# Cutting the last transform of a GFNet mixer at 94-token units instead of 512-token blocks, with a ring in front of the MLP

## The chip, the cores and the metric

One core of one Trainium2 chip runs the whole program. The metric is the device time of one execution in microseconds (us); lower is better. All numbers come from runs and their traces; where a page of the Trainium skill is drawn on, it is named.

## The reference, cut to what matters

```python
x: (8, 3008, 256)                 # 8 sequences, 3008 tokens, 256 channels
X = rfft(x, axis=1)
y = irfft(X * (filt_r + 1j * filt_i), n=3008, axis=1)      # GFNet mixing
t = y.reshape(24064, 256)
h = t @ w_in                                               # 256 -> 2048
g = h * clip(h + 3, 0, 6) / 6                              # hardswish
out = g @ w_out                                            # 2048 -> 256
```

The kernel computes the transforms as matrix products: 3008 = 47 x 64. The last product of the inverse transform takes one *unit* of 96 coefficients (in the partitions) x 256 channels and gives 94 tokens x 256 channels; a sequence has 32 such units. In the kernel's own token order the 24,064 tokens are 47 blocks of 512 for the MLP, which does its two products by a Strassen-like scheme of seven products. Everything is fp32; one product is two passes on TensorE, so two weight-load records (LDWEIGHTS) and two MATMUL records.

## The kernel before

A step is one of eight slices of the hidden width for one block: 376 steps. In two steps of a block the last transform of the *next* block is done (`n_unit`, one call for each half of the channels). It computes just the 512 tokens of that block, so the units at its edges are cut in two pieces:

```python
TOK = 94; BLK = 512
def pieces(k):                       # unit (b, j), first token r in it, n tokens, place in the block
    t = k * BLK
    while t < (k + 1) * BLK:
        u, r = divmod(t, TOK)
        n = min(TOK - r, (k + 1) * BLK - t)
        yield u // HC, u % HC, r, n, t - k * BLK
        t += n

def n_unit(k, dh):
    if dh == 0:
        st["xn", k] = xnp.tile([P, 2, 512], FP32, name="xn")
    ps = psF.tile([P, 512], FP32, name="psn", tag="f")
    for i, (_, _, r, n, o) in enumerate(pieces(k)):
        nc.tensor.matmul(ps[:, ds(o, n)], t4[k % 2][:, i, ts(dh, P)], wai[:, ds(r, n)], start=True, stop=True)
    x = st["xn", k]
    nc.scalar.activation(out=x[:, dh, :], in_=ps, func=AXT.Copy)
    if dh == 0:
        return
    ...                              # four GpSimd subtractions into xt, for the Strassen-like products

# in a step:                         (... cut)
up_1(k, p)                           # 3 products of 256 columns
do(True)                             # n_unit, or units of the other transforms
down(kd, pd, 1); up_2(k, p)          # 128-column and 256-column products by turns, and so on
```

`t4` is the stationary operand (its 128 columns are loaded for each piece) and `wai`, at most 94 columns, is what streams. `t4_load` brings the units of a block from a scratch tensor in HBM.

## Time and profile before

| what | value |
|---|---|
| median time | 2876.54 us at first, 2875.4 to 2877.6 in later rounds; single runs 2872.7 to 2880.2 |
| span of the profiled run | 2872.3 us |
| TensorE passes, those of the changed stage | 18,280, 1208 |
| bytes moved by DMA | 216.47 MB |
| first pass of the changed stage | at 135.7 us |

The prediction shows and reads the main lines. Names for the rest: a *pass* is one LDWEIGHTS with its MATMUL; of the tiles that TensorE writes, `psn` is that of the changed stage, `psf` those of the other transforms, `al` and `be` those of the MLP's first product and `po` that of its second.

### The profile page before, as it was taken

The page shows a single profiled execution, that of the slowest core. Times are in us where ns is not written, and L with a number is a line of the kernel's source. Part 1 is how long each engine was busy: PE and PEld are TensorE (multiplying, and loading weights), DVE is VectorE, ACT ScalarE, POOL GpSimd, SP SyncE. Part 2 cuts the span into 40 slices and gives each one's busy share as a digit, 9 for nine tenths or more (in the row PEclk, how much of TensorE's full clock was granted, in tenths as well). Part 3 has the DMA queues.
Part 4 walks back from the last instruction along what each step waited for, and adds up shares of the span by engine and source line. Part 5 has one row for each costly group of instructions (what it writes and reads, how often), then busy time and mean ns, then how long its engine had stood idle before and what let it go on. Part 6 is the DMA issues. An engine that isn't in the chain of part 4 may idle for free.

```text
span 2872.3 us, 47938 instructions
## 1 busy us (share of the span) xinstructions
PE 2745.6 (96%) x18280; PEld 2487.8 (87%) x18280; DVE 1991.8 (69%) x3492; ACT 1326.2 (46%) x2622; POOL 508.7 (18%) x836
## 2 busy tenths in 40 slices
PE   4569999999999999999999999999999999999997
PEld 1358988999989998899988999899998999999996
DVE  3697876677757776577766777667775677766665
ACT  1124445444454445544445444554445444444443
POOL 3274013200131001310023000321013100000000
PEclk9689999999999999999999999999999999999998
DMA  6543312421133222331223221242213421110100
GB/s 204 158 121 104 95 49 79 114 75 53 54 88 104 65 59 71 85 104 58 65 73 95 79 85 39 83 110 74 61 42 88 121 64 55 30 34 19 31 8 15
DMA packets 129036, 216.47 MB, mean 75 GB/s; under 512 B 26088, under 2 KB 87336, under 8 KB 128808
## 3 DMA queue, kind: packets, MB, share of 16 engines
q1 hardware_dynamic: 99784, 151.50, 18.6%
q0 software_dynamic: 23552, 55.62, 6.6%
q10 hardware_dynamic: 5472, 6.29, 0.6%
q8 instruction: 145, 2.38, 0.3%
q14 instruction: 83, 0.68, 0.1%
HBM read 138.33 MB, written 74.97 MB: 74 GB/s over the span
## 4 chain that ended last, share of the span: by engine, by line
PE 90%; DVE 4%; DMA 3%; POOL 1%; issue 1%; SPq 1%; ACT 1%; ACTq 0%; POOLq 0%; DVEq 0%
PE po L417 40%; PE al L341 22%; PE be L341 16%; PE psn L326 4%; PE psf L257 3%; PE psf L285 3%; PE psf L231 2%; DMA z_tmp<-t 1%; SPq L453 0%; DVE g L391 0%; DVE s L271 0%; DMA out_dram<-o 0%; DVE s L270 0%; POOL z_tmp L245 0%; DMA bits<-in_moe_w_out_dram 0%
## 5 line engine op out<-in xcount | busy, mean ns | idle before, releaser
L417 PEld LDWEIGHTS po<-w_out,g 128*128 128x128 f32 x10528 | 1408.8, 192 | 145.8 <-DVE g L399 31.3
L417 PE MATMUL po<-w_out,g 128*128 128x128 f32 x10528 | 1434.5, 277 | 25.8 <-DVE g L391 25.2
L386 ACT ACTIVATE r<-h,half_c 128x512 f32<-128x512 f32 x752 | 542.6, 722 | 341.8 <-DVE h L367 329.5
L391 DVE SCALAR_TENSOR_TENSOR g<-r,h 128x512 f32<-128x512 f32 x752 | 517.6, 688 | 257.0 <-ACT r L386 243.9
L341 PE MATMUL al<-xt,w_in 128*128 128x256 f32 x2256 | 677.4, 382 | 3.7 <-DVE h L372 2.1
L367 DVE TENSOR_TENSOR h<-be,s 128x512 f32<-128x512 f32 x376 | 259.8, 691 | 309.0 <-PE be L341 279.6
L341 PE MATMUL be<-xn,w_in 128*128 128x256 f32 x1504 | 447.8, 379 | 0.0
L341 PEld LDWEIGHTS al<-xt,w_in 128*128 128x128 f32 x2256 | 343.9, 193 | 6.8 <-issue 3.1
L341 PEld LDWEIGHTS be<-xn,w_in 128*128 128x128 f32 x1504 | 286.1, 190 | 38.9
L381 ACT ACTIVATE h<-al 128x256 f32<-128x256 f32 x376 | 144.4, 384 | 376.9 <-PE al L341 376.9
L372 DVE TENSOR_TENSOR h<-al,s 128x256 f32<-128x256 f32 x376 | 159.6, 425 | 193.1 <-PE al L341 192.8
L245 POOL DMA_DIRECT2D z_tmp<-t x448 | 226.2, 513 | 375.5 <-ACT t L234 366.9
L399 DVE TENSOR_TENSOR g<-g 128x512 f32<-128x512 f32 x376 | 262.6, 699 | 12.9
L362 ACT ACTIVATE s<-al 128x256 f32<-128x256 f32 x376 | 144.5, 384 | 201.9 <-PE al L341 201.9
L353 ACT ACTIVATE s<-be 128x256 f32<-128x256 f32 x376 | 144.4, 384 | 181.0 <-PE be L341 181.0
L341 PE MATMUL al<-xn,w_in 128*128 128x256 f32 x752 | 225.3, 381 | 0.5 <-ACT h L381 0.5
L341 PE MATMUL be<-xt,w_in 128*128 128x256 f32 x752 | 224.1, 380 | 0.0
L352 ACT ACTIVATE s<-al 128x256 f32<-128x256 f32 x376 | 144.4, 384 | 70.5 <-PE al L341 70.5
L398 DVE TENSOR_TENSOR g<-g 128x256 f32<-128x256 f32 x376 | 164.0, 436 | 12.8
L401 DVE TENSOR_TENSOR g<-g 128x256 f32<-128x256 f32 x376 | 161.0, 428 | 12.8
L326 PEld LDWEIGHTS psn<-wai,t 128*128 128x128 f32 x1208 | 152.0, 194 | 15.3 <-issue 10.6
L341 PEld LDWEIGHTS be<-xt,w_in 128*128 128x128 f32 x752 | 143.2, 190 | 19.4
(50 smaller groups left out, 1760.6 us busy)
## 6 DMA issues: line engine op xcount, KB each, us to landing
z_tmp<-t POOLq DMA_DIRECT2D x448, 48.0 KB, 2.1
t<-z_tmp SPq DMA_DIRECT2D x42, 512.0 KB
g_tmp<-t POOLq DMA_DIRECT2D x42, 512.0 KB, 3.4
xs<-in_x_dram SPq DMA_DIRECT2D x128, 128.0 KB
out_dram<-o SPq DMA_DIRECT2D x328, 47.0 KB
t<-g_tmp SPq DMA_DIRECT2D x96, 144.0 KB
ft<-in_filt_r_dram SPq DMA_DIRECT2D x96, 128.0 KB
ft<-in_filt_i_dram SPq DMA_DIRECT2D x96, 128.0 KB
```

Source lines behind the costliest of these rows:

```text
L245: q.dma_start(z[:, h, ds(c * XC + 2 * g, 2), :], t[p0:p0 + KH, h, :, :])
L326: nc.tensor.matmul(ps[:, ds(o, n)], t4[k % 2][:, i, ts(dh, P)], wai[:, ds(r, n)], start=True, stop=True)
L341: nc.tensor.matmul(ps, w_in[p][:, w, :], x, start=start, stop=stop, skip_group_check=True)
L362: nc.scalar.activation(out=s[:, 1, :], in_=al, func=AXT.Copy)
L367: nc.vector.tensor_tensor(out=st["h"][0].rearrange("p (a n) -> p a n", a=2), in0=be, in1=s, op=ALU.add)
L372: nc.vector.tensor_tensor(out=st["h"][1][:, 256:512], in0=al, in1=s5, op=ALU.add)
L386: nc.scalar.activation(out=r, in_=st["h"][i], func=AXT.Relu, bias=half_c, scale=1.0 / 6.0)
L391: nc.vector.scalar_tensor_tensor(out=st["g", k, p][:, o:o + 2, :].rearrange("p a n -> p (a n)"), in0=st["r", i], scalar=1.0, in1=st["h"][i ...
L398: v.tensor_tensor(out=g[:, G1, :], in0=g[:, G3, :], in1=g[:, G22, :], op=ALU.add)
L399: v.tensor_tensor(out=g[:, G3:G2 + 1:2, :], in0=g[:, G3:G1 + 1, :], in1=g[:, G11:G11 + 1, :].broadcast_to([P, 2, 256]), op=ALU.subtract)
L401: v.tensor_tensor(out=g[:, G4, :], in0=g[:, G12, :], in1=g[:, G2, :], op=ALU.subtract)
L417: nc.tensor.matmul(st["po", k][bank][:, part, u, :], g[:, a, ts(u, P)], w_out[p][:, w, :], start=(p == 0 and n in OPENS and u == 0), stop= ...
```

## The change

Its intent: cut at unit edges, so that no unit is loaded as weights twice, and let the MLP take its blocks of 512 out of a ring of three blocks into which chunks of up to five units (470 columns, within the 512 of a PSUM tile) are copied.

```diff
+NJ = 5
+RING = 3 * BLK
-    t4 = [const.tile([P, 7, D], FP32, name="t4%d" % i) for i in range(2)]
+    t4 = [const.tile([P, NJ, D], FP32, name="t4%d" % i) for i in range(2)]
+    xn = const.tile([P, 2, RING], FP32, name="xn")
 ...
+    chunks = [(b, j, min(NJ, HC - j)) for b in range(B) for j in range(0, HC, NJ)]
+    def n_unit(i, dh):
         ps = psF.tile([P, 512], FP32, name="psn", tag="f")
-        for i, (_, _, r, n, o) in enumerate(pieces(k)):
-            nc.tensor.matmul(ps[:, ds(o, n)], t4[k % 2][:, i, ts(dh, P)], wai[:, ds(r, n)], start=True, stop=True)
-        x = st["xn", k]
-        nc.scalar.activation(out=x[:, dh, :], in_=ps, func=AXT.Copy)
+        for q in range(chunks[i][2]):
+            nc.tensor.matmul(ps[:, ts(q, TOK)], t4[i % 2][:, q, ts(dh, P)], wai, start=True, stop=True)
+        t, n = token(i)
+        done = 0
+        while done < n:
+            o = (t + done) % RING
+            m = min(n - done, RING - o)
+            nc.scalar.activation(out=xn[:, dh, ds(o, m)], in_=ps[:, ds(done, m)], func=AXT.Copy)
+            done += m
+        if dh and (t + n) // BLK > t // BLK:
+            t_sums(t // BLK)                       # the four subtractions, as before
 ...
-        t4_load(0); t4_load(1)                     # (written here in one line)
-        for dh in range(2):
-            n_unit(0, dh)
+        for i in range(2):
+            t4_load(i)
+        for i in range(2):
+            for dh in range(2):
+                n_unit(i, dh)
 ...                                                # and the plan of the later chunks:
+            n_at[i] = s = (k - 1) * NP + (6 if head or k in used else 3)
+            at(max(stored, n_at[i - 2] + 1), t4_load, i)
```

The MLP's products read `xn[:, d, ts(k % 3, BLK)]`; the output stores are cut at the same places as before.

More of the change, by code (lines that the diff above doesn't have):

```diff
@@ L107 @@
     t3p = pool("t3p", 2)
-    xnp = pool("xnp", 2)
+    xtp = pool("xtp", 2)
     rp = pool("rp", 2)
@@ L292, in g_store @@
         q.dma_start(g_d[b, ts(c, TC), :, :].rearrange("k p d -> p k d"), st.pop(("t3", b, c)))
-    def pieces(k):
-        t = k * BLK
-        while t < (k + 1) * BLK:
-            u, r = divmod(t, TOK)
-            n = min(TOK - r, (k + 1) * BLK - t)
-            yield u // HC, u % HC, r, n, t - k * BLK
-            t += n
-    def t4_load(k):
-        slot = 0
-        found = []
-        for b, j, _, _, _ in pieces(k):
-            if found and found[-1][0] == b:
-                found[-1][2] += 1
-            else:
-                found.append([b, j, 1])
-        for b, j, n in found:
-            for h in range(2):
-                for ri in range(2):
-                    p0 = h * 64 + ri * 32
-                    nc.sync.dma_start(t4[k % 2][p0:p0 + KH, slot:slot + n, :],
-                                      g_d[b, :, ds(ri * NC + h * HC + j, n), :])
-            slot += n
@@ L321, in n_unit @@
-    def n_unit(k, dh):
-        if dh == 0:
-            st["xn", k] = xnp.tile([P, 2, 512], FP32, name="xn")
-        ps = psF.tile([P, 512], FP32, name="psn", tag="f")
-        for i, (_, _, r, n, o) in enumerate(pieces(k)):
-            nc.tensor.matmul(ps[:, ds(o, n)], t4[k % 2][:, i, ts(dh, P)], wai[:, ds(r, n)], start=True, stop=True)
-        x = st["xn", k]
-        nc.scalar.activation(out=x[:, dh, :], in_=ps, func=AXT.Copy)
-        if dh == 0:
-            return
-        t = xnp.tile([P, 4, 256], FP32, name="xt")
-        b11, b12, b21, b22 = (x[:, d, ts(h, 256)] for d in range(2) for h in range(2))
+    chunks = [(b, j, min(NJ, HC - j)) for b in range(B) for j in range(0, HC, NJ)]
@@ new lines, in token, with t4_load @@
+    def token(i):
+        b, j, n = chunks[i]
+        return b * N + j * TOK, n * TOK
+    def t4_load(i):
+        b, j, n = chunks[i]
+        for h in range(2):
+            for ri in range(2):
+                p0 = h * 64 + ri * 32
+                nc.sync.dma_start(t4[i % 2][p0:p0 + KH, 0:n, :], g_d[b, :, ds(ri * NC + h * HC + j, n), :])
+    def n_unit(i, dh):
+        ps = psF.tile([P, 512], FP32, name="psn", tag="f")
+        for q in range(chunks[i][2]):
[9 more added lines that the diff above has]
+            t_sums(t // BLK)
@@ L333, in n_unit, with xb, t_sums @@
+    def xb(k, d):
+        return xn[:, d, ts(k % 3, BLK)]
+    def t_sums(k):
+        t = xtp.tile([P, 4, 256], FP32, name="xt")
+        b11, b12, b21, b22 = (xb(k, d)[:, ts(h, 256)] for d in range(2) for h in range(2))
         for o, x0, x1 in ((0, b12, b11), (1, b22, t[:, 0, :]), (2, b22, b12), (3, b21, t[:, 1, :])):
@@ L343, in up_1 @@
     def up_1(k, p):
-        x, t = st["xn", k], st["xt", k]
+        t = st["xt", k]
         al = psU.tile([P, 256], FP32, name="al")
@@ L348, in up_1 @@
         s5 = hp.tile([P, 256], FP32, name="s5")
-        product(al, p, A11, x[:, 0, 0:256], start=True)
+        product(al, p, A11, xb(k, 0)[:, 0:256], start=True)
         product(be[:, 1, :], p, S1, t[:, 0, :], start=True)
-        product(be[:, 0, :], p, A12, x[:, 1, 0:256])
+        product(be[:, 0, :], p, A12, xb(k, 1)[:, 0:256])
         nc.scalar.activation(out=s[:, 0, :], in_=al, func=AXT.Copy)
@@ L356, in up_2 @@
     def up_2(k, p):
-        x, t = st["xn", k], st["xt", k]
+        t = st["xt", k]
         al, be, s, s5 = st["up"]
@@ L360, in up_2 @@
         product(al, p, S2, t[:, 1, :])
-        product(be[:, 1, :], p, S4, x[:, 1, 256:512], stop=True)
+        product(be[:, 1, :], p, S4, xb(k, 1)[:, 256:512], stop=True)
         nc.scalar.activation(out=s[:, 1, :], in_=al, func=AXT.Copy)
@@ L448, in out_5 @@
         o = st.pop(("o", k))[0].rearrange("p t u d -> p (t u) d")
-        for b, j, r, n, t in pieces(k):
-            while n:
-                h, a = divmod(r, NA)
-                m = min(NA - a, n, P - t % P)
-                nc.sync.dma_start(raw(out, b * N + a * NC + h * HC + j, [[NC * D, m], [1, D]]),
-                                  o[t % P:t % P + m, t // P, :])
-                r, t, n = r + m, t + m, n - m
+        t, end = k * BLK, (k + 1) * BLK
+        while t < end:
+            b, r = divmod(t, N)
+            j, r = divmod(r, TOK)
+            h, a = divmod(r, NA)
+            p = t % P
+            m = min(NA - a, P - p)
+            nc.sync.dma_start(raw(out, b * N + a * NC + h * HC + j, [[NC * D, m], [1, D]]),
+                              o[p:p + m, t % BLK // P, :])
+            t += m
     first = [b * N // BLK for b in range(B)]
@@ L514 @@
                         t2_load(0, c + TB, nc.gpsimd)
-        t4_load(0)
-        t4_load(1)
-        for dh in range(2):
-            n_unit(0, dh)
+        for i in range(2):
[3 more added lines that the diff above has]
+                n_unit(i, dh)
         for c in range(3):
@@ L523 @@
             at(i // 2, convert, 1)
-        for k in range(1, NBLK):
-            s = (k - 1) * NP
-            if k not in first:
-                if k > 1:
-                    at(s - 4, t4_load, k)
-                for dh in range(2):
-                    at(s + 3 + dh, n_unit, k, dh)
-            else:
-                at(s + (3 if k > first[1] else 4), t4_load, k)
-                for dh in range(2):
-                    at(s + 6 + dh, n_unit, k, dh)
+        n_at = {0: -2, 1: -2}
+        used = {}
+        stored = 0
+        for i in range(2, len(chunks)):
+            k = token(i)[0] // BLK
+            head = chunks[i][1] == 0
+            n_at[i] = s = (k - 1) * NP + (6 if head or k in used else 3)
+            used[k] = 1
+            if head:
+                stored = s - 3 + (k == first[1])
+            at(max(stored, n_at[i - 2] + 1), t4_load, i)
+            for dh in range(2):
+                at(s + dh, n_unit, i, dh)
         def places(n):
```

## The prediction

> **What bounds the kernel now.** I read the page's busy shares and slices first, then the windows of busy time by stage, then the waits of TensorE, then the groups with different shapes kept apart, and last the timeline and the chain around one run of the stage that is changed.
>
> ```profile
> PE 2745.6 (96%) x18280; PEld 2487.8 (87%) x18280; DVE 1991.8 (69%) x3492; ACT 1326.2 (46%) x2622; POOL 508.7 (18%) x836
> ...
> PE   4569999999999999999999999999999999999997
> ```
>
> TensorE is busy almost everywhere; the other engines have slack on average. The windows say where "almost" ends (columns: length, then busy us and instructions of each engine, granted clock, DMA share, GB/s).
>
> ```profile
> 0.00:142.00 142.00, 66.72 (x187) 33.89 (x188) 75.68 (x124) 18.33 (x31) 43.16 (x61) 0.85 0.61 182
> 142.00:217.00 75.00, 51.92 (x260) 38.69 (x258) 66.19 (x110) 21.95 (x44) 56.26 (x82) 0.82 0.42 121
> 217.00:1000.00 783.00, 776.35 (x5235) 707.68 (x5232) 558.41 (x973) 379.01 (x750) 145.20 (x249) 1.00 0.28 81
> 1000.00:2000.00 1000.00, 999.64 (x6789) 915.00 (x6787) 702.12 (x1239) 491.87 (x974) 170.52 (x296) 1.00 0.27 77
> 2000.00:2765.00 765.00, 765.00 (x5224) 711.60 (x5223) 531.47 (x944) 373.74 (x742) 89.25 (x144) 1.00 0.19 53
> ```
>
> Three stages: a prologue up to 142 us (the first sequence's transform) with TensorE half idle; 142 to 217 us, where VectorE is busy 66 of 75 us (it still converts the weights) and TensorE waits; and everything after, where TensorE has no idle time worth the name (7 us before 1000, 0.4 us from 1000 to 2765). From 217 us on a TensorE pass removed is time removed, and a wait appears only if something is made later by more than its slack. That DVE L391 is what TensorE waits for in the middle stage is shown by the waits of TensorE: 21.5 us there, 3.7 us after.
>
> The changed stage is the last inverse transform (`n_unit`), whose output `psn` feeds the MLP:
>
> ```profile
> L326 PE MATMUL psn<-wai,t 128*128 128x94 f32 x840 | 115.0, 283 | 9.7 <-DMA t<-g_tmp 9.7
> ...
> L326 PE MATMUL psn<-wai,t 128*128 128x10 f32 x8 | 1.2, 224 | 0.0
> ```
>
> (The last line is not needed for a sum; it shows what the change removes: 10-column products.) 1208 records are 604 products of two passes each. 840 passes have the full 94 columns, 368 are pieces cut by the 512-token block edge. What a pass costs is not its own duration (283 ns, pipelined) but the distance to the next start. The chain of waits, in time order, shows whole groups:
>
> ```profile
> 135.71 5.32 PE psn L326 x24
> ...
> 504.03 1.46 PE psn L326 x14
> ...
> 674.18 1.27 PE psn L326 x12
> ```
>
> Reading single starts inside them: full 94-column passes start every 111 to 112 ns, exactly as the 128-column passes of `po` do (mean 113); the distances of a group with pieces 92, 94, 94, 94, 94, 44 are 79, 112, 113, then 112 eight times apart from one 59 ahead of the last. So two narrow passes come some 30 to 80 ns cheaper per group, the others cost a weight load each, whatever their width.
>
> **What the Trainium skill says.** "TensorE: Matmul & The Clock Gate", section "LDWEIGHTS (loading the stationary operand)": a load takes about its column count over 1.2 GHz, and that is 107 ns for 128 columns; the trace's 111.5 ns agrees within 5 ns and explains why the width hardly matters. The same page's "Back-to-back issue gap" gives some 81 ns for a load and matmul pair at 128 columns; for these fp32 passes the trace has 112 to 113, and I use the trace. Its Part 1 on the clock gate says that a cold TensorE runs at half rate until about one window (3.4 us) of sustained work: the trace has a granted clock of 0.5 from 120.9 to 144.8 us, and the 24 passes at 135.7 us at 213 ns each; here the release came only 9 us after TensorE had begun. "Perfetto Trace Analysis", "Identifying the Most-Contended Engine", warns that matmul occupancy isn't closeness to the limit; that is why the 96% is not used as a measure and starts are.
>
> **The change part by part.**
>
> 1. *Cuts at units in place of blocks.* Each sequence's 32 units of 94 tokens go in chunks of 5, 5, 5, 5, 5, 5, 2: 56 chunks, 512 products, 1024 passes, all 94 wide. That is 184 passes fewer. The passes of blocks 1 to 46 took, start of group to start of what follows, 52 groups of 12 at 1.29 us and 40 of 14 at 1.49 us, 127.5 us in sum. Of this 0.6 us is one wait for a load and 0.75 us (8 times 0.09) belongs to the 64-row products that follow some groups: they cost the same extra after an MLP product. Left: 126.2 us. A new group of 10 passes should take 81 (its first, from the 79 of a 92-wide one) plus 9 x 112 = 1.09 us; a group of 4 passes 81 + 3 x 112 = 0.42 us. After the prologue there are 46 five-unit chunks and 8 two-unit ones, two groups (halves of D) each: 92 x 1.09 + 16 x 0.42 = 106.8 us. **Gain 19.4 us**, of which the two groups near 184 and 199 us (0.6 us) lie where VectorE is the bound and are worth nothing.
>
> 2. *Prologue.* Two chunks instead of one block must be done before the first MLP product: 40 passes in place of 24, at the cold 213 ns. **Loss 16 x 0.213 = 3.4 us.** It doesn't come back when block 1 needs less, because the next 70 us hang on VectorE, whose conversions begin behind the first MLP step and move with it. The second chunk's load is issued right behind the first (0.4 us per issue, four issues), so it should land during the first 4.3 us of passes.
>
> 3. *Evictions.* 94 ScalarE copies of 512 columns become 142: 112 chunk halves, 30 of them cut in two where the ring wraps (15 of 56 chunks). 512 columns take 597 ns and 256 take 384, so 171 ns are fixed; columns in sum are the same; 48 x 0.171 = 8.2 us more ScalarE work. ScalarE is 46% busy, a wrap delays one copy by 0.17 us, and the next copy that TensorE needs (`s`, L362) comes over a microsecond later. **0 us.**
>
> 4. *Loads.* 302 unit slots become 256, each 96 rows of 1 KB: 4.5 MB less of 216, in 224 issues instead of 216. DMA share is 0.2 to 0.3. The load of a chunk is issued as soon as its buffer is free (up to 15 steps ahead, formerly 7); a sequence's first chunk still comes 3 steps ahead. **0 us**, perhaps the 0.6 us of the one late load.
>
> 5. *GpSimd sums.* Still 188 subtractions. In ten blocks rather than seven they follow one step, about 7 us, ahead of use; they need a copy (0.6 us) and four times 0.73 us, 3.5 us. **0 us.**
>
> Sum: -19.4 + 0.6 + 3.4 = -15.4 us. 2876.5 - 15.4 = **2861 us**, 0.5% less.
>
> **Rivals.** (a) *A new wait in the ring.* Products of a block read what was written by up to two chunks, and a chunk overwrites the block two behind. If the dependencies were kept for the ring as a whole and not by region, each of 54 chunks could stall TensorE for a copy plus sums, some 3 to 5 us: +150 us or more, slower. Against it: the instruction order of the changed kernel shows the MLP's products waiting for no more semaphores than before, and the overwritten block was last read a step or more before the write. (b) *The late sums or the early loads stop an in-order queue.* SyncE now waits in its queue for the passes that free a buffer, and output stores and loads stand behind it; GpSimd issues `z_tmp` stores, eight in 4 us, beside the sums. If each of the 3 extra late blocks lost 2 us and a dozen loads 1 us, the gain would be nearly eaten: about 2872 to 2876. Against it: the old kernel has seven such blocks and no TensorE wait on GpSimd after 217 us, and the waiting loads stand in the queue less than a step. (c) *Fewer passes, same time*, if another engine were the true bound in the steps with `n_unit`. Steps without it run through with no TensorE gap, so the shorter step isn't caught by VectorE; I give this little. (d) *A prologue that hides its extra passes*: if the clock is released earlier, the loss is 1.8 us rather than 3.4 and the time 2859.
>
> **Range and chances.** The mechanism is counted, not guessed; what is unsure is the prologue (2 us each way), waits of a few us under (b), and the scatter of runs (2876.2 to 2879.9 before). I take 2855 to 2868. Faster by over 2% would need 58 us, three times all that can be removed; slower by over 2% needs (a).
>
> **What would show it.** TensorE records 18,096 in place of 18,280, all `psn` passes 94 wide and 1024 of them. `psn` groups of 10 in the chain with about 1.07 to 1.09 us, and none of 12 or 14. The prologue's passes as 40 in about 8.5 us, and the first MLP product near 144 rather than 141 us. ScalarE busy near 1334 us, GpSimd's count unchanged. TensorE idle after 217 us still under 10 us, with no GpSimd releaser. A larger idle sum naming `xn` copies or `xt` sums would make (a) or (b) right and the prediction wrong; groups of ten that take under 1.0 us or over 1.2 would break step 1.

## The result, and the profile after

Median 2857.90 us (2856.28 to 2859.84, 4 runs) against 2877.61 us (2876.24 to 2879.91, 4 runs): 19.7 us less. The ratio is 0.9931 (95% interval 0.9914 to 0.9948). The time lies in the predicted range, 3 us below the 2861 us foretold.

The page of the changed kernel, first its span and then its busy times:

```profile
span 2854.4 us, 47635 instructions
...
PE 2726.7 (96%) x18096; PEld 2469.4 (87%) x18096; DVE 1995.0 (70%) x3492; ACT 1331.6 (47%) x2670; POOL 511.7 (18%) x836
...
DMA packets 129323, 211.92 MB, mean 74 GB/s; under 512 B 26184, under 2 KB 87240, under 8 KB 129096
```

184 passes fewer, 48 ScalarE instructions more, GpSimd with the same count, 4.55 MB less moved: the counts that were foretold. (ScalarE is 5.4 us busier.) The groups of the last transform, shapes kept apart, and the waits of TensorE from 217 us on (columns: us in total, times, longest):

```profile
L316 PE MATMUL psn<-wai,t 128*128 128x94 f32 x1024 | 133.0, 278 | 9.2 <-DMA t<-g_tmp 9.2
```

```profile
PE po L417 <- DVE g L391: 4.1, 3, 2.5
PE al L341 <- DVE h L372: 2.1, 4, 1.2
PE psf L260 <- DVE s L274: 0.4, 1, 0.4
PE po L417 <- DVE o L443: 0.3, 1, 0.3
```

One shape is left where there were 47, and no wait on the ring's copies, on GpSimd or on a load appeared. The same list of the kernel before has 7.5 us in these stretches, this one 6.9; a wait of 0.4 us for a late `t4` load is gone. Its longest lines:

```profile
PE po L417 <- DVE g L391: 3.7, 3, 2.1
PE al L341 <- DVE h L372: 1.4, 3, 0.8
PE al L341 <- ACT s L362: 1.0, 1, 1.0
PE psf L257 <- DVE s L271: 0.4, 1, 0.4
PE psn L326 <- DMA t<-g_tmp: 0.4, 1, 0.4
```

The chain of waits, in time order, around one group after the change (start, length, what):

```profile
673.55 0.86 PE be L341 x4
674.41 1.09 PE psn L316 x10
675.50 0.47 PE po L417 x4
675.97 0.43 PE al L341 x2
```

A group of ten passes takes 1.09 us, as the prediction had it. The prologue, by windows of the trace (columns as in the prediction's windows), first before, then after:

```profile
135.70:140.80 5.10, 5.09 (x24) 5.10 (x25) 0.00 (x0) 0.60 (x1) 0.72 (x1) 0.50 0.85 190
140.80:144.80 4.00, 4.00 (x16) 2.15 (x15) 0.00 (x0) 1.36 (x3) 2.09 (x3) 0.50 0.47 111
144.80:149.30 4.50, 2.91 (x13) 1.28 (x9) 2.18 (x5) 2.50 (x6) 0.00 (x0) 1.00 0.29 86
```

```profile
136.70:145.30 8.60, 8.58 (x40) 8.60 (x41) 0.00 (x0) 1.69 (x3) 0.72 (x1) 0.50 0.81 204
145.30:146.10 0.80, 0.80 (x4) 0.71 (x4) 0.00 (x0) 0.52 (x1) 0.00 (x0) 0.53 0.31 65
146.10:152.20 6.10, 4.52 (x22) 2.10 (x21) 2.19 (x5) 3.32 (x9) 2.10 (x3) 1.00 0.52 143
```

The 24 passes became 40 and 5.1 us became 8.6, at the granted clock of 0.50 throughout. But the first MLP step, which ran 4.0 us at half clock before, now does so for 0.7 us only: 8.47 us from its first product to the next step's have become 6.84. (These are two single traces. Others of the same prologue have up to 3.6 us at half clock; see split_copies below.)

**A ruler for the rest.** The profiled runs of all these kernels differ by up to 5 us in when the changed stage begins, which is scatter of the part before it. So the trace is read in two stretches that don't contain it. The *head* goes from the first `psn` pass to the first MLP product of block 2 (step 16); the *body* from there to the start of the last TensorE pass. Both are differences of starts.

| kernel | head us | body us |
|---|---|---|
| before | 164.7 | 2550.9 |
| after | 166.7 | 2530.1 |
| change | +2.0 | -20.9 |

With the stage beginning 1.0 us later in this one run (136.7 against 135.7) that is the whole 17.9 us by which the two spans differ. The body repeated to 0.01 us in another run of the same kernel (2530.07), so tenths of a microsecond can be read from it.

### The profile page after: what moved, and what is told of

Same layout as the page of the kernel before. It is cut to its first block, busy times and chain, and to the rows that moved or that the text cites. A ratio compares the mean times of both kernels' runs of the same rounds, so it can differ in the third digit from the quotient of the medians.

```text
span 2854.4 us, 47635 instructions
## 1 busy us (share of the span) xinstructions
PE 2726.7 (96%) x18096; PEld 2469.4 (87%) x18096; DVE 1995.0 (70%) x3492; ACT 1331.6 (47%) x2670; POOL 511.7 (18%) x836
## 4 chain that ended last, share of the span: by engine, by line
PE 91%; DVE 5%; DMA 2%; issue 1%; ACT 1%; ACTq 0%; SPq 0%; POOL 0%; POOLq 0%; DVEq 0%
PE po L417 41%; PE al L341 22%; PE be L341 17%; PE psn L316 4%; PE psf L260 3%; PE psf L288 3%; PE psf L234 2%; DMA z_tmp<-t 1%; DVE g L391 0%; DVE s L183 0%; DVE s L192 0%; DVE s L194 0%; DVE s L181 0%; DVE g L398 0%; DVE s L274 0%
## 5 line engine op out<-in xcount | busy, mean ns | idle before, releaser
L334 POOL TENSOR_TENSOR xt<-xn 128x256 f32<-128x256 f32 x94 | 72.0, 766 | 508.1 <-ACT xn L322 508.0
```

## The experiments

The theory after the result: the gain is the number of passes, each worth one weight load of about 112 ns whatever its width; the prologue's extra passes cost something that is given back in part; copies, loads and sums cost nothing. All twelve kernels gave right results. The first four of the table, the next four, the next three and the last were each timed together, in five rounds, against nine runs of the kernel before; each of these batches ran on another chip, so medians are best compared within one, ratios across them.

| run | median us | ratio to before (95%) | head us | body us |
|---|---|---|---|---|
| after_again | 2856.61 | 0.9935 (0.9921 to 0.9948) | 166.7 | 2530.1 |
| add_passes | 2877.08 | 1.0007 (0.9995 to 1.0020) | 166.3 | 2549.4 |
| wide | 2853.87 | 0.9926 (0.9913 to 0.9938) | 163.8 | 2530.3 |
| long_head | 2865.76 | 0.9968 (0.9955 to 0.9980) | 176.5 | 2530.1 |
| split_copies | 2860.18 | 0.9936 (0.9924 to 0.9949) | 167.4 | 2530.5 |
| late_load | 2858.16 | 0.9938 (0.9925 to 0.9952) | 167.4 | 2530.1 |
| spread | 2857.72 | 0.9937 (0.9925 to 0.9950) | 167.5 | 2530.0 |
| spread_short | 2856.39 | 0.9926 (0.9914 to 0.9939) | 165.0 | 2529.6 |
| short_head | 2856.55 | 0.9931 (0.9918 to 0.9943) | 165.2 | 2529.6 |
| warm | 2855.63 | 0.9928 (0.9915 to 0.9940) | 161.6 | 2530.1 |
| warm_short | 2854.18 | 0.9923 (0.9910 to 0.9937) | 161.6 | 2529.6 |
| warm6_short | 2855.84 | 0.9924 (0.9910 to 0.9937) | 165.7 | 2529.6 |

**The base, once more.**

> The changed kernel once more, as the base for the runs beside it: 2856 to 2860 us, ratio to the kernel before 0.993.

2856.61 us, as expected.

**Is it the passes?** The number of passes is put back, and nothing else:

```diff
+        if i >= 2 and chunks[i][2] == NJ:
+            nc.tensor.matmul(ps[:, ts(NJ - 1, TOK)], t4[i % 2][:, NJ - 1, ts(dh, P)], wai, start=True, stop=True)
```

> Each five-unit group after the prologue repeats its last product: 92 products, 184 passes, as many as the change removed, all 94 wide, and nothing else. Theory (a pass costs one weight load, 112 ns): +184 x 0.112 = +20.6 us over the changed kernel, about 2878 us, so the whole gain is gone. Rival (the gain comes from better placed loads, evictions or sums, and passes are partly free): under +10 us.

The page of that run:

```profile
PE 2747.9 (96%) x18280; PEld 2490.1 (87%) x18280; DVE 1994.4 (69%) x3492; ACT 1329.8 (46%) x2670; POOL 509.2 (18%) x836
```

The pass count is that of the kernel before, and so is the time: 20.5 us more than after_again against 20.6 expected. In the body 176 of them stand, and it grew by 19.4 us: 110 ns each. The rival, that loads, copies or sums had brought the gain, falls: with all of those as in the changed kernel, the gain is gone.

**Is it the pass or its columns?** `wai` is padded with zeros to 128 columns and the next product overwrites what is too much:

```diff
-            nc.tensor.matmul(ps[:, ts(q, TOK)], t4[i % 2][:, q, ts(dh, P)], wai, start=True, stop=True)
+            nc.tensor.matmul(ps[:, ds(q * TOK, WID)], t4[i % 2][:, q, ts(dh, P)], wai, start=True, stop=True)   # WID = 128
```

> Each product runs over 128 columns in place of 94, 34 of them zeros that the next product overwrites; counts are the same. Theory (a pass costs its weight load, the width only shows in the first pass of a group): 108 groups x 28 ns = +3.0 us over the changed kernel. Rival (a pass costs its columns): 34/94 of some 107 us = +39 us.

Neither came. The rival's 39 us fall at once: 36% more columns cost 0.3 us in the body. But the theory's +3.0 us are a miss too. The groups did become 28 ns longer each, `psn` 2.9 us in the body, and the products *behind* them became shorter by 2.6 us (the `po` 1.9, the `psf` of the forward transform 0.7). And the whole run was 2.7 us faster: the head is 2.9 us shorter. Two things to explain, then; the next experiments do so.

**The 81 ns of a group's first pass.** In a group the first distance is 81 ns and the others 112. If that were a load hidden behind the 256-column pass ahead of it, then putting each product behind such a pass should pay:

```diff
+    def n_parts(i, dh):                      # the products of n_unit, one at a time, then the copy
 ...
         product(al, p, S2, t[:, 1, :])
+        next_part()
         product(be[:, 1, :], p, S4, xb(k, 1)[:, 256:512], stop=True)
+        next_part()
 ...                                          # and behind up_1 or an early unit, behind S3, behind A22
```

> The products of a chunk half stand one by one behind the 256-column MLP products of a step, in place of five in a row (not in the ten blocks whose sums follow one step ahead of use). If a pass behind a 256-column pass costs 81 ns because its load is hidden there, and the others 112, a five-product group of 1.09 us becomes five pieces of 0.19 us: 0.12 us less each, 82 groups, about -10 us against the changed kernel, 2848 us. Rival (the 81 ns is a matter of the record of the first pass alone, the load is not hidden): 0 us.

No gain: 2857.72 us, a body of 2530.0 us. The chain of waits in time order shows both sides of the account; in the first five rows the parts are spread over a step, the last three are of a step without the stage:

```profile
570.87 0.43 PE al L356 x2
571.30 0.19 PE psn L316 x2
571.50 0.46 PE be L356 x2
571.96 0.19 PE psn L316 x2
572.15 0.92 PE po L436 x8
...
578.77 0.43 PE al L356 x2
579.21 0.43 PE be L356 x2
579.64 0.89 PE po L436 x8
```

Two passes of `psn` take 0.19 us, 81 + 112 as foretold; but `be` and `po` right behind take 0.03 us more than in a step without them (0.46 against 0.43, 0.92 against 0.89). Over the body `psn` fell by 9.9 us, `po` rose by 7.7 and `be` by 2.9, the others changed by under 1. The short first distance is paid back by the second distance behind the group: 140 ns in place of 109 for `po`, 247 in place of 216 for 256 columns. With the payback counted, groups of the kernel before cost 1340 ns for 12 passes and 1563 ns for 14 (medians of 48 and 36 groups), those after 1086 + 31 = 1117 ns for 10: **111.7 ns a pass in all three**, the narrow pieces too. It also accounts for the 128-column version, whose first distance is 109 ns and whose payback is gone.

What the short distance is can be estimated from the traces: 256-column passes start every 216 ns and 512-column ones every 429 ns (in warm, below), or 0.84 ns a column. That puts 94 columns at 79 ns and 128 at 108 ns, beside the first distances of 81 and 109. So up to 128 columns fit into the 112 ns of a pass, which is as far as wide went; 256 do not. That each pass has a fixed cost whatever its width up to 128 is shown; that this cost is the weight load is argued, as no run changed the load alone.

**ScalarE's copies.** Each is cut at 235 columns: `m = min(n - done, RING - o, TOK * 5 // 2)`.

> Every copy of a chunk into the ring is cut into pieces of at most 235 columns, over 100 more ScalarE copies with some 0.17 us fixed cost each, about 18 us more ScalarE work. Theory (ScalarE is off the path): within 1 us of the changed kernel. Rival (the ring's extra copies eat part of the gain): +5 us or more.

96 copies more, 1337.4 us busy in place of 1330.1. The body grew by 0.4 us, and the ratio is that of after_again within 0.0001. The median is 3.6 us above that of after_again, on another chip; its five runs lie at 2856 to 2857 (two) and 2860 (three), those of late_load scatter in the same way, and I put no cause to that. An effect of 5 us or more is excluded in the body, where the copies stand.

The heads of split_copies and late_load are 0.7 us longer than that of after_again, and that of spread 0.8 us. Here the clock goes along: in these three traces it rises 2.6 to 3.6 us after the first MLP product, in after, after_again and add_passes, with the same prologue, 0.6 to 0.7 us after it. Two windows of late_load, whose first MLP product starts at 145.5 us:

```profile
136.90:145.50 8.60, 8.60 (x41) 8.60 (x41) 0.00 (x0) 1.69 (x3) 0.72 (x1) 0.50 0.87 196
145.50:149.00 3.50, 3.50 (x11) 2.03 (x14) 0.00 (x0) 1.33 (x3) 2.09 (x3) 0.50 0.18 44
```

In every trace here the stretches between two changes of the granted clock are multiples of 3.41 us (6.83, 10.24, 13.65, 23.89 and so on), and they begin at another point in each run. So tenths of a microsecond of a head depend on where such a step falls; no run tested it.

**The earlier loads.** `at(max(stored, n_at[i - 2] + 1, s - 7), t4_load, i)`.

> The loads of the chunks are issued at most 7 steps ahead, as in the kernel before, in place of up to 15. Theory (hidden either way): within 1 us of the changed kernel. Rival (the early loads either help, or hold up the in-order queue): a difference over 2 us in one direction.

Body 2530.07 us, exactly that of the changed kernel. Loading 15 or 7 steps ahead is the same.

**The prologue's price.** Its 20 products are done twice:

```diff
+            if i < 2:
+                nc.tensor.matmul(ps[:, ts(q, TOK)], t4[i % 2][:, q, ts(dh, P)], wai, start=True, stop=True)
```

> The 20 products of the prologue are done twice: 40 more passes before the first MLP product. The prediction's rule (passes in the prologue cost the cold 213 ns, and the shift lasts): +8.5 us. Rival (the granted clock rises at about the same moment, so most of the added passes run at 112 ns and the shift is smaller): +3 to +5.5 us, with the clock rising near 146 us in the trace while the passes are still running.

Windows of its trace:

```profile
137.90:155.10 17.20, 17.19 (x81) 17.20 (x81) 0.00 (x0) 1.69 (x3) 0.72 (x1) 0.50 0.44 108
155.10:157.20 2.10, 2.10 (x6) 1.70 (x6) 0.00 (x0) 0.95 (x2) 1.19 (x2) 0.51 0.37 115
157.20:162.60 5.40, 3.82 (x19) 1.49 (x17) 2.18 (x5) 2.88 (x7) 0.90 (x2) 1.00 0.42 118
```

The prediction's rule held, the rival fell: 17.2 us of uninterrupted passes (busy 17.19 of 17.20) and the clock stays at 0.50; it rises 2.1 us after the first MLP product. 40 passes more delayed that product by 8.54 us, or 213 ns each, and the time is 9.2 us up. So these 94-column passes did not raise the clock in this trace, and it isn't a fixed moment that does. In the wide run it was otherwise:

```profile
137.00:141.30 4.30, 4.30 (x20) 4.30 (x21) 0.00 (x0) 0.56 (x1) 0.00 (x0) 0.50 0.89 195
141.30:143.60 2.30, 2.30 (x23) 2.30 (x22) 0.00 (x0) 1.12 (x2) 0.30 (x1) 1.00 0.91 196
```

With 128 columns a pass the clock rises 4.3 us after the first of them, and the 40 passes take 6.6 us in place of 8.6. That is where the wide run's gain is: in the head.

**Less work in the prologue.** The first sequence's second chunk gets one unit, so that 24 passes suffice for block 0, as before; alone, and together with spread:

```diff
-    chunks = [(b, j, min(NJ, HC - j)) for b in range(B) for j in range(0, HC, NJ)]
+    chunks = [(0, 0, NJ), (0, NJ, 1)] + [(b, j, min(NJ, HC - j)) for b in range(B)
+                                         for j in range(0 if b else NJ + 1, HC, NJ)]
```

> The changed kernel with one unit instead of five in the first sequence's second chunk: 24 passes in the prologue as in the kernel before, and the 16 others later; the number of passes is the same. The prediction's prologue term (3.4 us) against 16 later passes at 112 ns (1.8 us, one part of them where VectorE is the bound): -1.6 to -3 us against the changed kernel. Rival (the prologue cost only about 1.9 us, as step 16 of the traces shows): 0 to -1.5 us.

> As spread, and the first sequence's second chunk has one unit instead of five, so that the prologue has 24 passes as in the kernel before and 16 passes more come later. The prediction's rule for the prologue: -3.4 + 16 x 0.1 = -1.8 us against spread. Rival (those passes cost about the same in both places): within 1 us of spread.

The first MLP product comes 5.7 us after the first pass in place of 8.6, and the head is 1.5 us shorter in short_head (165.2 against 166.7) and 2.5 us in spread_short against spread. The medians say 0.1 and 1.3 us less, the means of spread_short and spread, timed together, 3.1; the scatter is as large. Over all traces, the six with 40 cold passes have heads of 166.3 to 167.5 us and the four with 24 (before among them) heads of 164.7 to 165.7, or 1.8 us less in the mean. So the larger prologue's price is some 1.5 to 2.5 us, not 3.4; the head of short_head is at the upper end of the rival's figure and just short of the theory's.

**A warm clock.** TensorE is idle for 9 us before the first `psn` pass. Twelve products of 512 columns that nobody reads are put there, alone and with the short chunk; then six:

```diff
+        warm = psF.tile([P, 512], FP32, name="warm", tag="f")
+        for _ in range(12):
+            nc.tensor.matmul(warm, wa, w_in[0][:, 0:4, :].rearrange("p a m -> p (a m)"), start=True, stop=True)
```

> Twelve 512-column products whose result nobody reads run on TensorE while it waits for the first chunk's load (9 us idle before). If it is the cold clock that makes the prologue's 40 passes cost 213 ns, the clock rises before they start: 40 x 0.1 = 4 us earlier first MLP product (4.6 us after the first pass in place of 8.6), 3 to 4 us off the time, about 2853 us. Rival (the passes are slow for another reason, such as late data, or the clock falls again in them): 8.6 us stay, and no gain or a loss.

> Both: the clock raised before, and 24 passes in the prologue. First MLP product about 2.7 us after the first pass in place of 8.6; 4 to 6 us less than the changed kernel, about 2852 us, the fastest of all if so. Rival as in warm: no gain beyond the short chunk's.

> warm_short with six unread products in place of twelve: the trace of warm_short has the twelve taking 10.8 us, so that the first chunk's passes began 3 us later than without them. Six should end before the load lands. If so the first pass is back near 137 us, the first MLP product follows about 2.7 to 3.3 us later at the full clock, and the time falls by another 2 to 3 us against warm_short: 2851 to 2852 us. If the clock falls again before the passes start, they cost 213 ns and the time is that of the short head alone, about 2856 us.

In warm the 40 passes take 4.4 us in place of 8.6 and the head is 5.0 us shorter: the cold clock is what made them slow. But the twelve took 12.4 us, so that the stage began at 141.2 us in place of 137.2, and 1 us is left. I had misjudged them; a pass over 512 columns is 429 ns even at full clock, and the first ones took 853. The heads of warm and warm_short are both 161.6 us, though warm has 16 passes more before its first MLP product, which comes 1.1 us later after the first pass. So with a warm clock nothing of the larger prologue's delay was left at step 16 (one trace of each). In warm6_short the six ended too soon. Windows of warm_short and then of warm6_short (TensorE busy is the third number, the granted clock the third from the end):

```profile
129.00:137.00 8.00, 8.00 (x19) 3.57 (x19) 0.00 (x0) 0.60 (x1) 0.00 (x0) 0.93 0.61 194
137.00:147.00 10.00, 9.55 (x50) 5.77 (x48) 0.00 (x0) 3.19 (x8) 2.82 (x4) 1.00 0.72 192
```

```profile
129.00:137.00 8.00, 5.47 (x12) 2.05 (x10) 0.00 (x0) 0.18 (x1) 0.00 (x0) 0.93 0.61 192
137.00:147.00 10.00, 9.39 (x38) 7.35 (x38) 0.00 (x0) 2.28 (x6) 2.81 (x4) 0.50 0.67 192
```

With 5.5 us of work in the 8 us before 137 us the clock falls at 136.8 us, just ahead of the passes at 137.4, and these are cold again. A number between six and twelve was not tried. warm_short, at 2854.18 us and 0.9923, has the lowest ratio of all; against the changed kernel's 0.9931 and 0.9935 its interval is too wide to call it better.

## Why the prediction was right, and what was off

**What bounds it: right.** TensorE from 217 us on; removing passes removed time, and adding them gave it back (add_passes).

**Step 1, the passes: mechanism right, the size too small.** "A new group of 10 passes should take 81 ... plus 9 x 112 = 1.09 us" was met (1086 ns), and the old groups were read rightly, yet the difference between the groups isn't the whole gain. The term took the short first distance, and the shorter ones of narrow pieces ("two narrow passes come some 30 to 80 ns cheaper per group"), for a saving; the next passes pay it back. With 111.7 ns for every pass the 188 that the body lost are 21.0 us, and 20.9 were measured. In the body the groups, up to the start of what follows, shrank by 18.9 us (121.7 to 102.8), and the `po` and `psf` behind them by 1.9. The prediction had 18.8 us from 217 us on, a stretch that begins 83 us earlier (19.4 less 0.6 for two groups that it held to be worth nothing; by its own figures these two are 2 x (1.29 - 1.09) = 0.4 us).

**Step 2, the prologue: 3.4 us was right at the first MLP product and wrong in what stayed.** There the delay is 3.5 us (8.61 against 5.11). The sentence that failed is "It doesn't come back": at step 16 2.0 us are left in this trace. 1.6 us came back within the first MLP step, which used to run 4 us of its work at half clock and now 0.7. How much comes back there is in part luck of the run: in late_load, with the same prologue, 3.5 us of that step are at half clock, only 0.3 us comes back in it, and 2.7 us are left at step 16; the kernel before was traced once. In its size the 2.0 us is near rival (d)'s 1.8; its reason, an earlier release, isn't what happened: the clock rose 9.1 us after the first pass before and 9.3 us after. That added passes would cost 213 ns each was confirmed by long_head.

**Steps 3 to 5, copies, loads, sums: right.** split_copies and late_load changed the body by 0.4 and 0.0 us, and no TensorE wait on a copy or on GpSimd appeared. ScalarE's extra was 5.4 us, not 8.2; nothing hung on it.

**Rivals.** (a), a wait in the ring, and (b), a blocked queue, showed nowhere. (c), another bound in the steps with `n_unit`, is refuted by add_passes: each pass there counts in full.

**The sum.** Between the two traces, -20.9 + 2.0 = -18.9 us against the predicted -15.4; both errors had the same sign. The medians say -19.7 and, in five rounds, -18.8.

## What to carry to other kernels

Where each product has its own stationary operand and streams at most 128 columns, as far as these runs go, count passes, not columns (256 columns took 216 ns): cutting a tiling where the operand changes, and letting a ring absorb the mismatch with the consumer's blocks, removed 188 passes from the body at 112 ns each, without a new wait. Measure what a group of passes costs up to and including the passes behind it; a short distance inside may be paid back outside. And before a bounded stage begins, see which clock it begins with: that decides whether work moved there costs once or twice.

## What the Trainium skill lacked or had wrong

- "TensorE: Matmul & The Clock Gate", "LDWEIGHTS (loading the stationary operand)": 128 columns over 1.2 GHz are 107 ns, and the section doesn't say at which granted clock. Passes with their own load came every 111.7 ns at full clock here, at 94 and at 128 streamed columns and for groups with pieces as narrow as 2, and every 213 ns at a granted clock of 0.50. No experiment varied the stationary columns.
- The same page, "Back-to-back issue gap": about 81 ns for a load and matmul pair at 128 columns, without a data type. The fp32 passes here need 112; 81 ns is seen only as the first distance of a 94-column group, and 31 ns are paid back behind it, which no page mentions.
- The same page, Part 1 on the clock gate: some 3.4 us of sustained work release the clock. Here 17.2 us of passes with TensorE busy throughout, 94 columns each, left it at 0.50 (long_head); with 128 columns it rose after 4.3 us (wide), and in the eleven traces whose 256-column MLP products began at the cold clock it rose 0.6 to 4.0 us after the first of them. What the gate counts as work is not on the page, beyond how busy TensorE is and a remark on transposes; that it is the share of time in which columns stream would fit long_head and wide, but was only argued from them.
